# Linear attention with a routed expert layer in float32: two matmuls per chunk cut to 64x64 and 128x64 tiles of the array

## Chip, cores and metric

The kernel runs on one core of a Trainium2 chip. The metric is device time of one execution in microseconds (us). Before the change the median of 3 runs is 420.43 us (419.73 to 420.62).

## What is computed

Two layers follow each other. The first is causal linear attention with a decay per head (4 batches, 8 heads, 768 positions, 64 dimensions), with a state that goes from block to block; the second routes each of the 3072 tokens to one of 8 experts and runs that expert's two matrices.

```python
for b in range(nb):                                    # along the sequence
    intra = einsum('bhic,bhjc->bhij', qb, kb) * Dmask  # scores, with the decay
    intra = einsum('bhij,bhjd->bhid', intra, vb)
    inter = einsum('bhid,bhde->bhie', qb * lam_pow, kv_state)
    out[:, :, sl] = intra + inter
    kv_state = lam_block * kv_state + einsum('bhsd,bhse->bhde', kb * rev_pow, vb)
x = out, heads side by side                            # 3072 tokens of 512
e = argmax(x @ w_gate + modality_bias)                 # one expert for each token
y = gate * relu(x @ w1[e]) @ w2[e]
```

## The kernel before

**Attention.** The kernel takes the sequence in chunks of 128 positions: 6 per batch, 24 in all, and all 8 heads of a chunk together, as 4 pairs. In what follows a chunk has a number g from 0 to 23, and g % 6 is its place in the batch. The loop over g (`for g in range(0, ng + 2)`, from L730) is written as a pipeline, so that one turn works on three chunks. On TensorE (PE) a turn has five blocks of float32 matmuls, and the profile shows each such matmul as two passes:

- scores of chunk g (L224): keys times queries, for each pair and each head 64 rows of the array (one head's dimensions) and all 128 columns. Two heads go to two halves of the rows. The results are two tiles `s` in PSUM (three buffers in turn), one for the first heads of the pairs and one for the second.
- from the state, chunk g-1 (L262): 64x64 tiles, four side by side. Left out where g-1 begins a batch.
- outputs of chunk g-1 (L273): masked scores times values, 128 rows by 64 columns, two tiles side by side.
- carry of chunk g (L239): what the chunk adds to the state, 128 rows by 64 columns. Left out where g ends a batch.
- tokens of chunk g-2 (L285): the outputs are turned so that tokens stand in rows, and times the gate's weights, with all 128 rows and 128 columns of the array. The result goes to PSUM tiles `x` (two buffers).

VectorE (DVE) makes `pt`, the masked scores (L227, two per chunk, one for each tile `s`), `qd` and `kd`, decayed queries and keys (L204, L209), the state (L243, L248), the sum of the logits (`lg`, L289) and, once a batch, the routing. ScalarE (ACT) copies outputs and tokens out of PSUM (L275, L286). SyncE (SP) issues loads of 2 MB, one for two chunks (L182), into three buffers; the load of chunk pair n is issued when the outputs of chunk 2n-5 have read the last of the buffer that it goes to. Once a batch 7 small bf16 matmuls rank the tokens (`route_places`, L330 to L335), and once 1 counts tiles (L369).

The five blocks are written in this order, but a scheduler sets each engine's order from the dependencies and its own durations; an engine then takes its instructions in that order and waits at the one whose input is missing.

**Experts.** From some 116 us on the tokens of one expert are gathered in tiles of 256, and each float32 product is done as three matmuls of split operands (`three`, L588 to L592). Weights are split on ACT and DVE (`split`, L520, L521). The last chunk's tokens block stands among the first matmuls of the experts.

Of the kernel before, what the change touches and what calls it, by code (L numbers as in the profile page):

```python
# [15 lines left out]
P = 128  # L16
# [6 lines left out]
E, DM, F = 8, 512, 1024  # L23
# [15 lines left out]
def linear_attention_moe(tc, qkv, lam, modality, wg, mbias, w1, w2, out):  # L39
    nc = tc.nc  # L40
    with ExitStack() as ctx:
# [78 lines left out]
        iw = const.tile([P, NP, P + E], F32, name="iw")  # L120
# [50 lines left out]
        halves2 = [slice(hl * D, (hl + 1) * D) for hl in range(2)]  # L171
# [17 lines left out]
        def loaded(g):  # L189

            t = halves[g // HB][:, :, g % HB]
            kt, qt = (t[:, i].rearrange("p (a t) -> p a t", a=NP) for i in range(2))
            return kt, qt, t[:, 2], t[:, 3]
# [23 lines left out]
        def scores(g):  # L217
            kt, qt, vt, kn = loaded(g)
            pts = []
            sps = [ps.tile([P, NP, P], F32, name="s", bufs=3),  # L220
                   ps.tile([P, NP, P], F32, name="x", bufs=2) if g == 1 else ps.tile([P, NP, P], F32, name="s", bufs=3)]
            for p in range(NP):
                for hl, r in enumerate(halves2):
                    nc.tensor.matmul(sps[hl][:, p, :], kt[r, p, :], qt[r, p, :], start=True, stop=True)  # L224
            for hl in range(2):
                pt = work.tile([P, NP, P], F32, name="pt", bufs=4)
                op = nc.vector.tensor_tensor(out=pt, in0=sps[hl], in1=dk[:, hl], op=ALU.mult)  # L227
                pts.append(pt)
            return pts, op
# [48 lines left out]
        def tokens(g, xt, lg):  # L278
            c = g % NC
            xn = work.tile([P, NP, P + E], F32, name="xn", bufs=4)  # L280
            for hf in range(2):
                xp = ps.tile([P, 2, 256], F32, name="x", bufs=2)
                for j in range(2):
                    p = hf * 2 + j
                    nc.tensor.matmul(xp[:, j, : P + E], xt[:, p, :], iw[:, p, :], start=True, stop=True)  # L285
                copies.append(nc.scalar.copy(out=xn[:, 2 * hf : 2 * hf + 2, :], in_=xp[:, :, : P + E]))  # L286
            nc.scalar.dma_start(out=xs[g * P : (g + 1) * P, :].rearrange("t (p d) -> t p d", p=NP),
                                in_=xn[:, :, :P])
            logits.append(nc.vector.tensor_reduce(out=lg[:, c, :], in_=xn[:, :, P:].rearrange("p q e -> p e q"),  # L289
                                                  axis=AX, op=ALU.add))  # L290
# [439 lines left out]
        for g in range(0, ng + 2):  # L730
# [4 lines left out]
            if g < ng:  # L735
                st1[g], masked = scores(g)
# [15 lines left out]
            if g >= 2:  # L752
                b, c = divmod(g - 2, NC)
                if c == 0:
                    lgs[b] = work.tile([P, NC, E], F32, name="lg", bufs=2)
                tokens(g - 2, st2.pop(g - 2), lgs[b])
                if routed is not None:
                    slots = route_places(*routed)
                    routed = None
                if c == NC - 1:  # L760
                    routed = (b, *route(b, lgs.pop(b)))
# [30 lines left out]
        hl = [work.tile([P, 2, TT], F32R, name=f"hl{i}", tag=t, bufs=3) for i, t in enumerate(("qd", "qd", "kd", "kd"))]  # L792
# [154 lines left out]
```

## Time and profile before

| | |
|---|---|
| median of 3 runs | 420.43 us |
| profiled execution | 419.86 us |
| its span, first to last instruction | 418.1 us |
| PE busy | 404.6 us (97% of the span) |
| DVE busy | 245.9 us (59%) |
| ACT busy | 188.4 us (45%) |
| GpSimd (POOL) busy | 100.0 us (24%) |
| read from HBM, written | 90.97 MB, 13.68 MB |
| stage of attention | up to some 116 us |

The page lists each engine's busy time; a matmul's end is modelled, so a busy PE says that it always had work, not that the work was dense. How dense it is shows in the timeline: it gives each block's start, and the distance from one block's start to the next can be set against the number of passes in the block. PE's granted clock is 0.996 of full speed over the span.

### The profile page before, as it was taken

The page shows a single profiled execution, that of the slowest core. Times are in us where ns is not written, and L with a number is a line of the kernel's source. Part 1 is how long each engine was busy: PE and PEld are TensorE (multiplying, and loading weights), DVE is VectorE, ACT ScalarE, POOL GpSimd, SP SyncE. Part 2 cuts the span into 40 slices and gives each one's busy share as a digit, 9 for nine tenths or more (in the row PEclk, how much of TensorE's full clock was granted, in tenths as well). Part 3 has the DMA queues.
Part 4 walks back from the last instruction along what each step waited for, and adds up shares of the span by engine and source line. Part 5 has one row for each costly group of instructions (what it writes and reads, how often), then busy time and mean ns, then how long its engine had stood idle before and what let it go on. Part 6 is the DMA issues. An engine that isn't in the chain of part 4 may idle for free.

```text
span 418.1 us, 9536 instructions
## 1 busy us (share of the span) xinstructions
PE 404.6 (97%) x3665; PEld 356.4 (85%) x3666; DVE 245.9 (59%) x487; ACT 188.4 (45%) x298; POOL 100.0 (24%) x110
## 2 busy tenths in 40 slices
PE   8999999999979999999999999999999999999993
PEld 4687888888879888689898989899998989898982
DVE  4594967788369952168393745638190927456240
ACT  1213343233378151258392736546381927365330
POOL 3110143522540741050322030212121120300001
PEclk9999999999999999999999999999999999999998
DMA  4999989899940039101206567711111020200101
GB/s 145 396 335 381 349 295 330 277 313 318 393 141 3 2 109 401 55 18 45 75 28 184 183 210 250 230 51 52 52 33 69 2 76 27 67 27 2 52 1 48
DMA packets 35093, 63.01 MB, mean 151 GB/s; under 512 B 7381, under 2 KB 21213, under 8 KB 35040
## 3 DMA queue, kind: packets, MB, share of 16 engines
q1 hardware_dynamic: 17056, 43.08, 29.8%
q0 software_dynamic: 4768, 12.69, 9.1%
q10 hardware_dynamic: 13216, 6.56, 5.3%
q8 instruction: 30, 0.49, 0.5%
q14 instruction: 23, 0.19, 0.2%
HBM read 90.97 MB, written 13.68 MB: 250 GB/s over the span
## 4 chain that ended last, share of the span: by engine, by line
issue 44%; PE 22%; DMA 13%; POOL 8%; DVE 6%; POOLq 3%; SPq 3%; ACT 1%; DVEq 0%; ACTq 0%
PE s L224 6%; PE x L285 5%; DMA load<-in_qkv_dram 5%; PE o L273 5%; DMA idx<-inv 4%; POOL out_dram L666 4%; POOL xg L548 3%; DMA xg<-xs,idx 3%; POOLq L844 2%; PE o L262 2%; PE kv L239 2%; DVE w1l L521 1%; SPq L565 1%; DVE w2l L521 1%; PE s L592 1%
## 5 line engine op out<-in xcount | busy, mean ns | idle before, releaser
L588 PE MATMUL s<-xh,w1h 128*128 128x256 f32 x384 | 107.4, 280 | 0.8 <-ACT xh L520 0.8
L592 PE MATMUL s<-xh,w1l 128*128 128x256 f32 x384 | 107.4, 280 | 0.8 <-DVE w1l L521 0.8
L591 PE MATMUL s<-xl,w1h 128*128 128x256 f32 x384 | 107.2, 279 | 0.0
L521 DVE TENSOR_TENSOR w1l<-raw,w1h 128x1024 fp32r<-128x1024 f32 x48 | 58.0, 1218 | 72.6 <-ACT w1h L520 72.6
L588 PE MATMUL o<-w2h,hh 128*128 128x512 f32 x192 | 75.8, 395 | 0.0
L592 PE MATMUL o<-w2h,hl 128*128 128x512 f32 x192 | 74.9, 390 | 0.0
L591 PE MATMUL o<-w2l,hh 128*128 128x512 f32 x192 | 74.8, 390 | 0.0
L588 PEld LDWEIGHTS s<-xh,w1h 128*128 128x128 f32 x384 | 72.2, 188 | 1.6 <-ACT xh L520 1.0
L592 PEld LDWEIGHTS s<-xh,w1l 128*128 128x128 f32 x384 | 72.2, 188 | 1.2 <-DVE w1l L521 1.2
L591 PEld LDWEIGHTS s<-xl,w1h 128*128 128x128 f32 x384 | 72.2, 188 | 0.4
L521 DVE TENSOR_TENSOR w2l<-raw,w2h 128x1024 fp32r<-128x1024 f32 x48 | 58.3, 1217 | 2.0 <-ACT w2h L520 2.0
L520 ACT CAST w1h<-raw 128x1024 fp32r<-128x1024 f32 x48 | 50.0, 1055 | 20.6 <-PE s L591 19.8
L520 ACT CAST w2h<-raw 128x1024 fp32r<-128x1024 f32 x48 | 50.1, 1045 | 0.0
L665 ACT ACTIVATE y<-o,idx 128x512 f32<-128x512 f32 x20 | 13.8, 690 | 75.9 <-PE o L592 45.9
L666 POOL DMA_INDIRECT out_dram<-y,idx x20 | 20.3, 1014 | 114.8 <-ACT y L665 99.4
L607 DVE SCALAR_TENSOR_TENSOR hl<-s,hh 128x512 fp32r<-128x512 f32 x48 | 32.8, 684 | 22.3 <-ACT hh L606 22.3
L592 PEld LDWEIGHTS o<-w2h,hl 128*128 128x128 f32 x192 | 36.0, 188 | 7.6
L591 PEld LDWEIGHTS o<-w2l,hh 128*128 128x128 f32 x192 | 36.1, 188 | 7.2
L588 PEld LDWEIGHTS o<-w2h,hh 128*128 128x128 f32 x192 | 36.1, 188 | 7.1
L548 POOL DMA_INDIRECT xg<-xs,idx x20 | 24.6, 1228 | 72.7 <-PE x L581 68.8
L275 ACT COPY xt<-o 128x256 f32<-128x256 f32 x48 | 17.8, 372 | 49.7 <-PE o L273 45.6
L606 ACT ACTIVATE hh<-s 128x512 fp32r<-128x512 f32 x48 | 28.7, 597 | 19.8 <-PE s L592 19.6
(190 smaller groups left out, 487.4 us busy)
## 6 DMA issues: line engine op xcount, KB each, us to landing
raw<-in_w_dram SPq DMA_DIRECT2D x104, 512.0 KB
load<-in_qkv_dram SPq DMA_DIRECT2D x11, 2048.0 KB
xs<-xn ACTq DMA_DIRECT2D x24, 256.0 KB
load<-in_qkv_dram SPq DMA_DIRECT2D x4, 512.0 KB
spare<-in_w_dram SPq DMA_DIRECT2D x4, 512.0 KB
w1h<-in_w_dram SPq DMA_DIRECT2D x4, 512.0 KB
inv<-pad SPq DMA_DIRECT2D x2, 196.0 KB
inv<-pad SPq DMA_DIRECT2D x2, 192.0 KB
```

Source lines behind the costliest of these rows:

```text
L224: nc.tensor.matmul(sps[hl][:, p, :], kt[r, p, :], qt[r, p, :], start=True, stop=True)
L273: mm = nc.tensor.matmul(op[half][place(p, hl), i, :], vt[:, (2 * p + hl) * D : (2 * p + hl + 1) * D], pts[hl][:, p, :], start=(c == 0 and ...
L285: nc.tensor.matmul(xp[:, j, : P + E], xt[:, p, :], iw[:, p, :], start=True, stop=True)
L520: cp = nc.scalar.copy(out=hi, in_=src)
L521: df = nc.vector.tensor_tensor(out=lo, in0=src, in1=hi.bitcast(F32), op=ALU.subtract)
L548: last = nc.gpsimd.indirect_dma_start(out=(to or xg)[t][:m], out_offset=None, in_=xs[:rows, :], in_offset=bass.IndirectOffsetOnAxis(ap=idx ...
L588: mm = nc.tensor.matmul(out, ah, bh, start=first, stop=False)
L591: nc.tensor.matmul(out, ah, bl, start=False, stop=False)
L592: return nc.tensor.matmul(out, al, bh, start=False, stop=last)
L606: act = nc.scalar.activation(out=hh[i], in_=hp, func=AF.Relu)
L607: nc.vector.scalar_tensor_tensor(out=hl[i], in0=hp, scalar=0.0, in1=hh[i].bitcast(F32), op0=ALU.max, op1=ALU.subtract)
L666: sc = nc.gpsimd.indirect_dma_start(out=out, out_offset=bass.IndirectOffsetOnAxis(ap=idx[:, t, 0:1], axis=0), in_=y, in_offset=None, bound ...
```

## The change

Two loops get one more level. The scores of one head are no longer one matmul of 64 rows and 128 columns, but two of 64 rows and 64 columns, for the two halves of the key positions; so a chunk's scores have 16 matmuls in place of 8, on four tiles of the array. The tokens block is cut the same way along its columns: 8 matmuls of 128 rows and 64 columns in place of 4 of 128 by 128. The number of columns that each matmul streams (128 and 136) stays. Operands, results and everything else in the program stay too; the two new lines move the line numbers behind them by one and two.

```diff
             for p in range(NP):
                 for hl, r in enumerate(halves2):
-                    nc.tensor.matmul(sps[hl][:, p, :], kt[r, p, :], qt[r, p, :], start=True, stop=True)
+                    for s in halves2:
+                        nc.tensor.matmul(sps[hl][s, p, :], kt[r, p, s], qt[r, p, :], start=True, stop=True)
...
                 for j in range(2):
                     p = hf * 2 + j
-                    nc.tensor.matmul(xp[:, j, : P + E], xt[:, p, :], iw[:, p, :], start=True, stop=True)
+                    for r in halves2:
+                        nc.tensor.matmul(xp[r, j, : P + E], xt[:, p, r], iw[:, p, :], start=True, stop=True)
```

The tilings of a turn, block by block, are 64x128, 64x64, 128x64, 128x64 and 128x128 before; with the change they are 64x64, 64x64, 128x64, 128x64 and 128x64.

The scheduler's order changes in two ways. The first is on PE, at the routing of a batch. Before, from the tokens of chunk 6 on (a row is a group of matmuls, out<-in and the output's shape; `load` is q, k and v):

```order
L285 MATMUL x<-iw,xt 128x136 x4
L224 MATMUL s<-load 128x128
L330 LDWEIGHTS lowb
L330 MATMUL x<-oh,lowb 128x48
L333 LDWEIGHTS onesb
L333 MATMUL x<-ohsum,onesb 128x48
...
L335 MATMUL x<-oh,onesb 128x8
L224 MATMUL s<-load 128x128 x7
L262 MATMUL o<-qd,state_117 64x128 x8
```

Now:

```order
L287 MATMUL x<-iw,xt 64x136 x8
L332 LDWEIGHTS lowb
L332 MATMUL x<-oh,lowb 128x48
L335 LDWEIGHTS onesb
L335 MATMUL x<-ohsum,onesb 128x48
...
L337 MATMUL x<-oh,onesb 128x8
L225 MATMUL s<-load 64x128 x16
L263 MATMUL o<-qd,state_117 64x128 x8
```

The routing (and the count of L369) has moved from behind the first matmul of the scores to directly behind the tokens.

The second is on DVE: of the two `kd` of a newly loaded chunk pair, the second has moved forward. Before, from the masked scores of chunk 9 on; the first `kd` is that of chunk 12 and waits for the load of chunks 12 and 13, the second that of chunk 13, and the masked scores between them are those of chunk 10:

```order
L227 TENSOR_TENSOR pt<-s,dk 128x512 x2
L204 TENSOR_TENSOR qd<-load,pq 128x512
L248 TENSOR_TENSOR state_116<-faded,kv 128x256
L289 TENSOR_REDUCE lg<-xn 128x8
L209 TENSOR_TENSOR kd<-load,dk 128x512
L227 TENSOR_TENSOR pt<-s,dk 128x512 x2
L204 TENSOR_TENSOR qd<-load,pq 128x512
L209 TENSOR_TENSOR kd<-load,dk 128x512
L248 TENSOR_TENSOR state_117<-faded,kv 128x256
```

Now:

```order
L228 TENSOR_TENSOR pt<-s,dk 128x512 x2
L204 TENSOR_TENSOR qd<-load,pq 128x512
L249 TENSOR_TENSOR state_116<-faded,kv 128x256
L291 TENSOR_REDUCE lg<-xn 128x8
L209 TENSOR_TENSOR kd<-load,dk 128x512 x2
L228 TENSOR_TENSOR pt<-s,dk 128x512 x2
L204 TENSOR_TENSOR qd<-load,pq 128x512
L249 TENSOR_TENSOR state_117<-faded,kv 128x256
```

Both `kd` now stand ahead of the masked scores of chunk 10. The same holds at the load of chunks 18 and 19, ahead of the masked scores of chunk 16; there the order before was

```order
L404 TENSOR_SCALAR deltaA<-ntA 1x8
L384 TENSOR_TENSOR tmpA<-tri,ntA 1x64
L209 TENSOR_TENSOR kd<-load,dk 128x512
L385 TENSOR_REDUCE endsA<-tmpA 1x8
L227 TENSOR_TENSOR pt<-s,dk 128x512
L388 TENSOR_TENSOR pastA<-sidx,endsA 1x16
L227 TENSOR_TENSOR pt<-s,dk 128x512
```

and is now

```order
L209 TENSOR_TENSOR kd<-load,dk 128x512
L406 TENSOR_SCALAR deltaA<-ntA 1x8
L386 TENSOR_TENSOR tmpA<-tri,ntA 1x64
L209 TENSOR_TENSOR kd<-load,dk 128x512
L387 TENSOR_REDUCE endsA<-tmpA 1x8
L228 TENSOR_TENSOR pt<-s,dk 128x512
L390 TENSOR_TENSOR pastA<-sidx,endsA 1x16
L228 TENSOR_TENSOR pt<-s,dk 128x512
```

The second `kd` and two small instructions of the tile list have come between the waiting `kd` and the masked scores. At the load of chunks 8 and 9 `qd` and `kd` of chunk 9, which stood behind the masked scores of chunk 7, stand ahead of them now, and at the loads of chunks 14 and 15 and of 20 and 21 the waiting `qd` stands ahead of the masked scores of chunk 12 and 18, behind which it stood. The orders of ACT, POOL and SP are what they were.

## Rows read from the trace of the kernel before

**Rows 1.** The page of the profile: busy time, share of the span and instructions of each engine, and the line of PE by slice (tenths of busy time; 40 slices of 10.45 us).

```profile
PE 404.6 (97%) x3665; PEld 356.4 (85%) x3666; DVE 245.9 (59%) x487; ACT 188.4 (45%) x298; POOL 100.0 (24%) x110
...
PE   8999999999979999999999999999999999999993
```

**Rows 2.** The view by stretch, two stretches of the attention stage: length, busy time of each engine in us (with the number of instructions), granted clock of PE, share of time in which the DMA engines were busy, GB/s.

```profile
36.60:46.30 9.70, 9.70 (x162) 8.59 (x162) 7.60 (x15) 3.04 (x8) 1.00 (x2) 1.00 1.03 365
46.30:55.60 9.30, 9.30 (x157) 8.17 (x153) 7.93 (x29) 2.97 (x9) 3.50 (x5) 1.00 0.97 337
```

**Rows 3.** The timeline of PE, two steady chunks, the second by its first block alone: start in us, length in us, engine, line, operation, tiles and shape. A row takes in all instructions of a block (x16 is 8 float32 matmuls of two passes); the next row starts where the next block starts. The last row is the block with which the chunk after ends.

```profile
62.01 1.16 PE L224 MATMUL s<-load 64*128 64x128 f32 x16
63.10 0.67 PE L262 MATMUL o<-qd,state 64*64 64x128 f32 x16
63.70 1.09 PE L273 MATMUL o<-pt,load 128*64 128x128 f32 x16
64.62 0.64 PE L239 MATMUL kv<-load,kd 128*64 128x64 f32 x16
65.18 1.19 PE L285 MATMUL x<-iw,xt 128*128 128x136 f32 x8
66.31 1.16 PE L224 MATMUL s<-load 64*128 64x128 f32 x16
...
70.01 1.16 PE L224 MATMUL s<-load 64*128 64x128 f32 x16
```

**Rows 4.** What passes cost without a switch between them, and whether weight loads lie beside them: the timeline of PE in the thin tile of 32 rows (four column tiles), the group of that line among the groups by line (busy us, mean ns of one), and the timeline of the weight loads for the block of outputs that starts at 63.70.

```profile
179.98 1.95 PE L644 MATMUL o<-spare,hnt 128*32 128x128 f32 x64
...
L644 PE MATMUL o<-spare,hnt 128*32 128x128 f32 x64 | 2.0, 274 | 0.1
...
63.69 0.85 PEld L273 LDWEIGHTS o<-pt,load 128*64 128x64 f32 x16 [0.17 <-issue]
```

**Rows 5.** A chunk with routing matmuls: the timeline of PE, and of ACT for the copies out of the tokens block that starts at 47.77.

```profile
48.89 0.49 PE L224 MATMUL s<-load 64*128 64x128 f32 x2
49.31 0.20 PE L330 MATMUL x<-oh,lowb 128*128 128x48 bf16 x1
...
53.87 1.16 PE L224 MATMUL s<-load 64*128 64x128 f32 x16
...
48.54 0.85 ACT L286 COPY xn<-x 128x272 f32<-128x272 f32 x2
```

**Rows 6.** The timeline of DVE where it waits for a load of q, k and v (in brackets: us idle before, and what ended it), and the rows behind.

```profile
42.30 0.69 DVE L204 TENSOR_TENSOR qd<-load,pq 128x512 f32<-128x512 f32 x1 [2.00 <-DMA load<-in_qkv_dram]
...
43.63 1.28 DVE L227 TENSOR_TENSOR pt<-s,dk 128x512 f32<-128x512 f32 x2
...
56.74 0.69 DVE L209 TENSOR_TENSOR kd<-load,dk 128x512 f32<-128x512 f32 x1 [2.13 <-DMA load<-in_qkv_dram]
57.34 1.28 DVE L227 TENSOR_TENSOR pt<-s,dk 128x512 f32<-128x512 f32 x2
...
81.51 0.70 DVE L209 TENSOR_TENSOR kd<-load,dk 128x512 f32<-128x512 f32 x1 [0.49 <-DMA load<-in_qkv_dram]
82.13 0.20 DVE L385 TENSOR_REDUCE endsA<-tmpA 1x8 f32<-1x64 f32 x1
82.26 0.67 DVE L227 TENSOR_TENSOR pt<-s,dk 128x512 f32<-128x512 f32 x1
...
82.94 0.67 DVE L227 TENSOR_TENSOR pt<-s,dk 128x512 f32<-128x512 f32 x1
...
86.41 1.27 DVE L227 TENSOR_TENSOR pt<-s,dk 128x512 f32<-128x512 f32 x2
...
90.88 0.69 DVE L204 TENSOR_TENSOR qd<-load,pq 128x512 f32<-128x512 f32 x1 [0.45 <-DMA load<-in_qkv_dram]
```

**Rows 7.** The timeline of PE: the first block of chunk 6, and the blocks that the rows of the group before lead to (scores of chunk 8; outputs of chunks 7, 10, 16 and 18).

```profile
36.59 1.16 PE L224 MATMUL s<-load 64*128 64x128 f32 x16 [0.98 <-DMA load<-in_qkv_dram]
...
44.59 1.16 PE L224 MATMUL s<-load 64*128 64x128 f32 x16
...
46.28 1.09 PE L273 MATMUL o<-pt,load 128*64 128x128 f32 x16
...
59.86 1.09 PE L273 MATMUL o<-pt,load 128*64 128x128 f32 x16
...
85.80 1.09 PE L273 MATMUL o<-pt,load 128*64 128x128 f32 x16
...
93.34 1.09 PE L273 MATMUL o<-pt,load 128*64 128x128 f32 x16
```

**Rows 8.** The timeline of SP: the issues of the loads of chunk pairs 6 and 9.

```profile
47.42 0.37 SPq L182 DMA_DIRECT2D load<-in_qkv_dram  x1
...
72.84 0.37 SPq L182 DMA_DIRECT2D load<-in_qkv_dram  x1
```

**Rows 9.** The way from attention into the experts, by engine: PE at the last tokens block, the ACT copy of its second half, the DVE split behind it, and PE as it takes that up.

```profile
119.47 0.73 PE L285 MATMUL x<-iw,xt 128*128 128x136 f32 x4 [0.99 <-DVE xl L521]
...
123.96 0.38 PE L592 MATMUL s<-xh,w1l 128*128 128x256 f32 x1 [0.38 <-DVE w1l L521]
...
120.94 0.39 ACT L286 COPY xn<-x 128x272 f32<-128x272 f32 x1 [0.32 <-PE x L285]
...
122.69 1.22 DVE L521 TENSOR_TENSOR w1l<-raw,w1h 128x1024 fp32r<-128x1024 f32 x1
```

## The prediction

> **What bounds the kernel now.** I read the page first: PE is busy for 97% of the span, in every slice but two for 90% or more [rows 1]. That alone does not say that PE sets the time, since a stalled stream of matmuls also counts as busy. [...] The timeline of PE then shows how dense the work is: one turn of the loop takes 66.31 - 62.01 = 4.30 us, and a turn without the state block 70.01 - 66.31 = 3.70 us [rows 3]. Last, the timeline of DVE shows where loads end a wait: at 42.30, 56.74, 81.51 and 90.88 DVE starts the moment that a load of q, k and v lands [rows 6].
>
> **What a switch of tiling costs.** The longest run of passes without a switch has 64 on four tiles: (1.95 - 0.274) / 63 = 26.6 ns per pass of 128 columns [rows 4], so 53.2 ns on two tiles and 106 on one. By that a turn's passes take: scores 16 x 53.2 = 0.85, state 16 x 26.6 = 0.43, outputs 0.85, carry (64 columns) 0.43, tokens 8 x 106 x 136/128 = 0.90; together 3.46. The turn's 4.30 leaves 0.84 for four switches, 0.21 each. A second way: the turn without the state block is 0.60 shorter [rows 3]; its passes are 0.43, and it has one switch less, so a switch is 0.17. Where the tiling stays, from outputs to carry, the distance is 0.92 against passes of 0.85; where it changes, from state to outputs, 0.60 against 0.43. I take 0.18, nearer to the second, which compares two turns alike in all else; bounds 0.17 and 0.21.
>
> **The change, part by part.** *Scores and tokens themselves.* Scores become 32 passes on four tiles, 32 x 26.6 = 0.85; tokens 16 on two, 0.90. The passes cost what they cost before. I add 0.02 per turn for scores: their row has 16 passes from 62.01 in 1.16, outputs 16 in 1.09 [rows 3]. As to the weight loads, twice as many: in the outputs block 16 of them take 0.85 us, as long as the passes beside them [rows 3, 4], so they hide. [...]
>
> *Switches per turn.* 4 become 2: a full turn saves 2 x 0.18 + 0.02 = 0.38. A turn without the state block has 3 before and 2 now: 0.20. A turn without the carry goes from outputs to tokens, a switch before and none now: 4 to 2, again 0.38. The three routings and the one count lose one switch (0.18), but now stand directly behind tokens and need the `x` buffer whose copy starts at 48.54 and is half of 0.85 long, so free at 48.97, against 48.89 where PE could start [rows 5]: 0.18 - 0.08 = 0.10 each.
>
> *Until chunk 6: nothing.* Its scores start at 36.59 after 0.98 of waiting for a load [rows 7]; I take that landing as fixed, so that what is saved earlier turns into a longer wait.
>
> *Chunk 6 to the outputs of chunk 10: lost.* DVE takes its instructions in order, and the new order puts `qd` and `kd` of two chunks ahead of the masked scores behind them. At 42.30 four of them (0.60 each, the distance of two starts at 56.74 and 57.34) and the small `lg` (0.12) come first: masked scores of chunk 7 start at 44.8, not 43.63, and the first is done 0.68 later, at 45.5 [rows 6]. The third matmul of chunk 8's scores writes the buffer that this frees. Behind it lie 28 passes (0.75), state (0.43) and a switch (0.18): outputs of chunk 7 start at 46.9, not 46.28 [rows 7]. Their end issues load 6 (47.42 now) [rows 8], which comes up to 0.6 later; with the queue full, 0 to 0.6 of it may reach the landing, and I take all: 57.3 in place of 56.74. Then two `kd` (1.20), the masked scores (0.68) and again 0.75 + 0.43 + 0.18: outputs of chunk 10 start at 60.5, against 59.86: 0.7 late.
>
> *Then up to the outputs of chunk 16.* Saved: 0.18 for the rest of turn 11, 4 x 0.38 for turns 12 and 14 to 16, 0.20 for turn 13, 0.20 for turn 17 up to its outputs block, and 2 x 0.10 for a routing and the count: 2.3, so 1.6 ahead. But load 9, issued behind the outputs of chunk 13 (72.84) [rows 8], is only some 0.26 earlier by then (-0.7 + 0.18 + 0.38 + 0.20 + 0.20), and lands at 81.25. Behind it now lie 0.75 (as from 81.51 to 82.26), the second `kd` 0.60 and two small ones, 0.13 each by the row of `endsA`; the masked scores start at 82.9, end at 83.5 [rows 6], and 0.75 + 0.43 + 0.18 later the outputs of chunk 16 start at 84.9. That is 0.9 ahead of 85.80 [rows 7], not 1.6.
>
> *To the end of attention.* The masked scores of chunk 17 come 3.47 after the second of chunk 16 (82.94 to 86.41 [rows 6]), now 0.60 less, and hold PE for some 0.15. Saved: 0.18, then turns 18 to 23 with 5 x 0.38 + 0.20, the last state block's 0.18 and one routing 0.10: 2.56. So attention ends 0.9 + 2.56 - 0.15 = 3.3 earlier.
>
> *Into the experts.* The last tokens block stands among 128x128 matmuls, and its new tiling adds four switches. Two of them lie ahead of the copy at 120.94, on which the sum of logits, the routing's first steps and the split at 122.69 follow, for which PE waits at 123.96 [rows 9]: 0.36 lost; the others fall into that wait. From there on PE is full [rows 1] and everything it waits for hangs on its own progress, so the rest moves along.
>
> **Sum.** 3.3 - 0.36 = 2.9 saved. The profiled execution took 419.86, its span 418.1; 419.86 - 2.9 = 417.0. The median of the runs lies 0.57 above it: **417.5**. Its own range: the far end if loads 9 and 10 come no earlier (outputs of chunk 18 then start at 90.88 + 0.60 + 0.68 + 0.75 + 0.18 = 93.1, 0.25 ahead of 93.34 [rows 6, 7], and 0.18 + 4 x 0.38 + 0.18 + 0.10 - 0.36 = 1.6 follow: 1.9 saved, 418.5); and 416.5 with load 6 not delayed (0.5, as it brings load 9 that much forward) and 14 switches at 0.21 behind load 9 (0.4).
>
> **Rivals.**
> *The loads follow the faster PE and DVE keeps up.* Then all turns from chunk 6 on save: 15 x 0.38 + 3 x 0.20 + 0.18 + 0.40 = 6.9, less 0.36: 413.9. For it: each load is issued by PE's own outputs. Against: the DMA engines are busy for 0.97 and more of these stretches [rows 2], and the new DVE order waits earlier. Chance 0.15.
> *Not the tiling costs, but each change of block.* Five blocks stay five, nothing is gained, and the DVE waits stay hidden in the slack: 420.4. For it: the blocks differ in more than their tiling. Against: outputs to carry is 0.92 with 0.07 over its passes, a new block at nearly no cost [rows 3]. Chance 0.10.
> *Slower: four tiles do not run side by side for a whole scores block.* The tiles of one head now share rows of queries and come as neighbours. If they went two at a time, at the 53.2 ns of two tiles, scores would take 1.70: 0.85 more against 0.38 less, some 9 us over 18 turns: 429. It decides from (0.85 + 0.38) / 32 = 38 ns per pass on. Against it: 26.6 ns held for 64 passes whose four tiles share all rows [rows 4], and the state block takes 0.60 [rows 3]. [...] Chance 0.06.
>
> **How the numbers follow.** The forecast has 0.69, of which 0.10 is the case of unmoved loads. Some 0.84 us (0.2%) is what a measurement of this kernel can tell from no change, so faster means under 419.6. Faster: 0.82 (0.67 from the forecast, 0.15 from the first rival); within: 0.12 (0.10 from the second rival, 0.02 from the forecast); slower: 0.06. The range leaves out the second and third rivals and a little (0.04) of the first: 414.6 to 419.4.
>
> **What would show it.** Right: a full turn of 3.9 us in the timeline of PE with switches only ahead of scores and of outputs; scores in 0.85 us; new waits of PE for `pt` in the scores of chunks 8, 11 and 17; attention over by 113. Wrong: turns of 3.9 with no such waits (first rival), turns of 4.3 (second), scores of over 1.2 us (third), or a wait of PE on the gathered rows of the first expert tile, which must be there 3 us earlier.

## The result, and the profile after

The forecast was wrong. The changed kernel took 422.81 us in the median of 13 runs, the kernel before 420.12 us beside it: a ratio of 1.0064 (95% interval 1.0039 to 1.0088), slower, where 417.5 us was forecast. In a second comparison, on another chip, it was 426.41 against 420.41 us, 1.0154 (1.0118 to 1.0189). The profiled execution took 421.71 us. Medians are of all executions, ratios leave out slow ones at a lower granted clock, among them one of the kernel before at 665.29 us (clock 0.557) and one of chunk_pads_tokens (below) at 611.12 (0.604).

The page after, against [rows 1]: busy time and instructions of the engines, PE's busy time by slice, and the granted clock by slice.

```profile
PE 399.3 (95%) x4242; PEld 351.2 (84%) x4242; DVE 246.6 (59%) x487; ACT 188.0 (45%) x298; POOL 100.2 (24%) x110
...
PE   8897889899979999999999999999999999999994
...
PEclk9999999999989999999999999999999999999999
```

PE has 577 more matmul records and 5 us less busy time. It now has holes in the first third, the attention stage, and a lower clock at the way into the experts (0.84 of full speed in the slice from 115.5 us on).

The blocks themselves do what was forecast. PE in a steady turn, against [rows 3]:

```profile
50.41 1.10 PE L225 MATMUL s<-load 64*64 64x128 f32 x32
51.34 0.62 PE L263 MATMUL o<-qd,state 64*64 64x128 f32 x16
51.88 1.09 PE L274 MATMUL o<-pt,load 128*64 128x128 f32 x16
52.81 0.64 PE L240 MATMUL kv<-load,kd 128*64 128x64 f32 x16
53.27 1.10 PE L287 MATMUL x<-iw,xt 128*64 128x136 f32 x16
54.30 1.10 PE L225 MATMUL s<-load 64*64 64x128 f32 x32
```

A turn takes 54.30 - 50.41 = 3.89 us, 0.41 less than before. The time went into what lies between the turns. PE's waits from 20 to 126 us (engine and line that waited, for what, us in total, times, longest):

```profile
PE s L225 <- DVE pt L228: 3.6, 4, 1.6
PE s L225 <- DMA load<-in_qkv_dram: 3.0, 2, 2.4
PE o L274 <- issue: 1.7, 1, 1.7
PE x L583 <- DMA xg<-xs,idxA: 1.6, 1, 1.6
```

Before, the same stretch had no wait for `pt`, none for gathered rows and none with the releaser "issue" (PE waits, and nothing in the profile holds it); loads cost 1.4. Where these waits lie, in the timeline of PE, against [rows 7]:

```profile
37.15 1.10 PE L225 MATMUL s<-load 64*64 64x128 f32 x32 [2.35 <-DMA load<-in_qkv_dram]
...
46.20 0.98 PE L225 MATMUL s<-load 64*64 64x128 f32 x26 [1.27 <-DVE pt L228]
...
47.66 1.09 PE L274 MATMUL o<-pt,load 128*64 128x128 f32 x16
...
60.27 0.98 PE L225 MATMUL s<-load 64*64 64x128 f32 x26 [1.65 <-DVE pt L228]
...
61.73 1.09 PE L274 MATMUL o<-pt,load 128*64 128x128 f32 x16
...
83.65 0.66 PE L274 MATMUL o<-pt,load 128*64 128x128 f32 x8 [1.70 <-issue]
...
87.91 1.09 PE L274 MATMUL o<-pt,load 128*64 128x128 f32 x16
...
118.86 0.98 PE L583 MATMUL x<-ident,xg 128*128 128x128 f32 x7 [1.60 <-DMA xg<-xs,idxA]
```

SP issues loads 6, 9 and 11 later, the first two against [rows 8] (load 11 before: 90.78):

```profile
48.80 0.37 SPq L182 DMA_DIRECT2D load<-in_qkv_dram  x1
...
74.14 0.37 SPq L182 DMA_DIRECT2D load<-in_qkv_dram  x1
...
93.86 0.38 SPq L182 DMA_DIRECT2D load<-in_qkv_dram  x1
```

And PE's granted clock falls behind the wait for gathered rows (first row: a stretch of 4 us, columns as in [rows 2]). The second row is the same stretch of a second profile of the kernel before: there is no such wait there, and the clock falls too.

```profile
120.00:124.00 4.00, 3.58 (x21) 2.44 (x22) 1.29 (x2) 1.30 (x5) 2.07 (x2) 0.64 0.70 201
```

```profile
120.00:124.00 4.00, 4.00 (x23) 4.00 (x24) 2.21 (x9) 2.77 (x5) 1.12 (x2) 0.60 0.61 170
```

The first expert tile scales its output at 141.95, 2.78 us later than in the first profile before and 1.48 later than in the second (140.47); the next one is 1.89 later than in the first, and so it stays to the end.

### The profile page after: what moved, and what is told of

Same layout as the page of the kernel before. It is cut to its first block, busy times and chain, and to the rows that moved or that the text cites. A ratio compares the mean times of both kernels' runs of the same rounds, so it can differ in the third digit from the quotient of the medians.

```text
span 420.0 us, 10687 instructions
## 1 busy us (share of the span) xinstructions
PE 399.3 (95%) x4242; PEld 351.2 (84%) x4242; DVE 246.6 (59%) x487; ACT 188.0 (45%) x298; POOL 100.2 (24%) x110
## 4 chain that ended last, share of the span: by engine, by line
issue 45%; DMA 23%; PE 9%; DVE 8%; POOL 8%; SPq 3%; POOLq 3%; ACT 0%; DVEq 0%
DMA load<-in_qkv_dram 12%; DMA idx<-inv 4%; POOL out_dram L668 4%; POOL xg L550 3%; DMA xg<-xs,idx 3%; PE s L225 3%; POOLq L846 2%; PE o L274 2%; PE x L287 2%; DMA xg<-xs,idxA 2%; DVE w1l L523 2%; SPq L567 1%; DMA raw<-in_w_dram 1%; PE o L263 1%; DVE kd L209 1%
```

## Experiments

Three theories. **A**: the new DVE order makes PE wait for masked scores behind loads, so loads are issued later, and all behind them. **B**: PE runs out of instructions, since a turn has 48 float32 matmuls where it had 36 (a third more; the 1.6 times in the expectation below is wrong). **C**: a late load 3 was an accident of the transfers. Medians are compared with the kernel before in the same comparison. "Without a releaser" sums PE's waits with the releaser "issue" from 20 to 115 us of one profile, or to the end of attention where that comes earlier; the last column is the start of the first transpose of the first expert tile, the end of attention.

| run | matmuls, switches per turn | median us (runs) | ratio to before (interval) | without a releaser, us | attention ends |
|---|---|---|---|---|---|
| before, first profile | 36, 4 | | | 0 | 116.19 |
| before_again | 36, 4 | 420.22 (1) | | 0 | 116.56 |
| the change, first profile | 48, 2 | 422.81 (13) | 1.0064 (1.0039 to 1.0088) | 1.7 | 116.93 |
| change_again | 48, 2 | 426.41 (6) | 1.0154 (1.0118 to 1.0189) | 3.4 | 119.91 |
| dve_order_before | 48, 2 | 424.21 (6) | 1.0107 (1.0070 to 1.0143) | 2.3 | 118.32 |
| masked_first | 48, 2 | 422.06 (12) | 1.0037 (1.0004 to 1.0070) | 3.7 | 117.15 |
| old_masked_first | 36, 4 | 421.09 (12) | 1.0022 (1.0000 to 1.0044) | 0.8 | 118.91 |
| scores_only | 44, 3 | 421.07 (11) | 1.0039 (1.0015 to 1.0063) | 0 | 118.24 |
| scores_masked_first | 44, 3 | 422.34 (12) | 1.0042 (1.0013 to 1.0072) | 1.9 | 121.42 |
| tokens_only | 40, 3 | 420.17 (12) | 1.0000 (0.9970 to 1.0030) | 0 | 116.34 |
| tokens_masked_first | 40, 3 | 419.95 (12) | 0.9980 (0.9956 to 1.0003) | 0.7 | 115.41 |
| no_loads_old | 36, 4 | 449.70 (4) | 1.0711 (1.0679 to 1.0744) | 0 | 114.97 |
| no_loads_new | 48, 2 | 442.54 (4) | 1.0531 (1.0493 to 1.0569) | 0.7 | 107.03 |
| chunk_loads_old | 36, 4 | 417.73 (12) | 0.9939 (0.9919 to 0.9960) | 0 | 114.72 |
| chunk_loads_new | 48, 2 | 421.87 (12) | 1.0034 (1.0009 to 1.0059) | 2.3 | 118.20 |
| chunk_pads_old | 36, 4 | 422.67 (12) | 1.0011 (0.9973 to 1.0050) | 0 | 114.76 |
| chunk_pads_scores | 44, 3 | 423.01 (12) | 1.0014 (0.9981 to 1.0047) | 2.5 | 115.28 |
| chunk_pads_tokens | 40, 3 | 414.40 (6) | 0.9846 (0.9808 to 0.9885) | 0.2 | 111.48 |
| chunk_pads_new | 48, 2 | 419.62 (12) | 0.9960 (0.9927 to 0.9993) | 6.6 | 115.90 |

### The changed kernel a second time

No edit.

> The changed kernel as it is, for a second profile and a second set of times. Every theory: 421.5 to 423.5 us. What it tells: which of the stretches that the first profile of the changed kernel lost are lost each time. Theory A (the new DVE order makes PE wait for masked scores, the loads of q, k and v are issued later, and all behind them) says that the waits of 1.3 us in the scores of chunk 8 and of 1.6 us in those of chunk 11 are there again, within 0.3. Theory B (PE runs out of instructions, since the change has 1.6 times as many per chunk) says that a wait of PE like the 1.7 us in the outputs of chunk 15, for which the profile shows no releaser, is there again, there or in another block of attention. Theory C (an accident of the transfers: load 3 came 0.6 us late) says that load 3 lands before 36.7 us this time, and that what follows is earlier by as much.

The wait in the scores of chunk 8 was there (1.5 us), that of chunk 11 only 0.3. Load 3 landed in time (scores of chunk 6 at 36.18), as C says, and the run was slower all the same: C does not explain the loss. What came back is the stall without a releaser, in more pieces. PE in the state block of chunk 15 and its outputs:

```profile
80.96 0.45 PE L263 MATMUL o<-qd,state 64*64 64x128 f32 x3 [0.37 <-issue]
81.69 0.46 PE L274 MATMUL o<-pt,load 128*64 128x128 f32 x4 [0.28 <-issue]
82.41 0.27 PE L274 MATMUL o<-pt,load 128*64 128x128 f32 x1 [0.27 <-issue]
83.12 0.55 PE L274 MATMUL o<-pt,load 128*64 128x128 f32 x4 [0.44 <-issue]
83.83 0.37 PE L274 MATMUL o<-pt,load 128*64 128x128 f32 x1 [0.16 <-issue]
84.55 0.89 PE L274 MATMUL o<-pt,load 128*64 128x128 f32 x5 [0.34 <-issue]
```

The block's inputs are there, since its first passes have run, and it takes from 81.69 to 85.07 where [rows 3] has 0.92. Its pieces start 0.71 to 0.72 us apart. Meanwhile the transfers have thinned out (DMA share, last column but one, of 0.49, then 0.12 and 0.05), so these holes are not explained by transfer engines that are full at that moment. Behind them the granted clock falls:

```profile
82.00:83.00 1.00, 0.41 (x5) 0.00 (x0) 0.00 (x0) 0.00 (x0) 0.69 (x2) 1.00 0.49 128
83.00:84.00 1.00, 0.72 (x5) 0.42 (x5) 0.77 (x1) 0.00 (x0) 0.97 (x2) 0.86 0.12 35
84.00:85.00 1.00, 0.66 (x5) 0.46 (x5) 1.00 (x4) 0.12 (x1) 0.62 (x1) 0.50 0.05 5
...
84.00:88.00 4.00, 3.65 (x47) 3.28 (x50) 4.00 (x15) 1.27 (x4) 1.81 (x2) 0.61 0.26 61
```

### DVE's order: dve_order_before, masked_first, old_masked_first

```diff
# dve_order_before (the changed kernel): kd and qd behind masked scores as in the kernel before
+        pt_of, hold = {}, {9: 7, 13: 10, 14: 12, 19: 16, 20: 18}
...
+            if after is None and g in hold:
+                after = pt_of[hold[g]]
...
+            pt_of[g] = op
# masked_first (the changed kernel), old_masked_first (the kernel before)
-            if 1 <= g < ng - 1:
-                st0[g + 1] = prepare(g + 1)
...
                 st1[g], masked = scores(g)
+            if 1 <= g < ng - 1:
+                st0[g + 1] = prepare(g + 1, None if g + 1 == 18 else masked)
```

> The changed kernel, with the order on DVE held as it was before the change at the five places where it had moved: kd and qd of chunks 9, 13, 14, 19 and 20 behind the masked scores of chunks 7, 10, 12, 16 and 18. PE, ACT, POOL and SP keep the orders of the changed kernel. Theory A: the waits of PE for masked scores go (1.27, 1.65 and 0.39 us), each load behind them is issued 1 to 1.5 us earlier, and the kernel takes 2 to 3 us less than the changed one: 419.5 to 421, no slower than the kernel before. Theory B (instructions): it takes what the changed kernel takes, 422 to 423.5. The forecast's own sum without the lost stretches (the switches alone) would be 416.5 to 418.

> The changed kernel, with kd and qd of each chunk behind the masked scores of the chunk before it, so that DVE never waits for a load ahead of masked scores that PE waits for (kd of chunk 18 alone stays where it was, since SP's order would move otherwise). Orders of PE, ACT, POOL and SP as in the changed kernel. Theory A: outputs of chunks 7, 8, 10, 13 and 14 no longer hang on the load that lands in their turn, loads 6 and 9 are issued earlier than in the kernel before, and the time is another 1 to 2 us under that of the run with the DVE order of before: 417.5 to 420. A rival to that, transfers at their rate (the DMA engines are busy for 0.97 and more of the stretch before the change, so that an earlier issue brings no earlier landing): as the run with the order of before, within 0.5 us. Theory B: 422 to 423.5.

> The kernel before with its own tilings, and the same edit of the DVE order as in the run masked_first: the two have the same DVE order to the instruction, so they differ by the tilings alone. What the tilings are worth once DVE's order is no matter: if a switch of tiling costs what the forecast says and PE sets the pace, this run is 2 to 3 us slower than masked_first. If the loads set the pace, the two are alike within 0.7 us. If the doubled instructions cost (theory B), this run is the faster of the two by 1 us or more. Against the kernel before: 0 to 2 us less.

With the order of before, the change took 2.20 us less, which is not clear of noise (the intervals, 1.0070 to 1.0143 and 1.0118 to 1.0189, overlap); PE still waited 1.8 us for `pt` there. With masked scores first it took 4.35 less, clear of noise, and PE had no wait for `pt`, while it stood as long without a releaser as in change_again (3.7 against 3.4). So A is a part. But neither came under the kernel before, and with one DVE order in both the old tilings took 421.09 and the new 422.06, a difference within the noise: the switches saved nothing that stayed. masked_first has 3.7 us without a releaser. Its times follow the mean granted clock: three runs at 0.997 and 0.998 took 419.6 to 420.5, five at 0.979 to 0.989 took 423.0 to 426.0.

### Each half alone: scores_only, tokens_only, scores_masked_first, tokens_masked_first

The diff of the change, one half of it; the last two with the edit of masked_first.

> The kernel before with the first half of the change: scores on four 64x64 tiles, tokens as before on the whole array. A turn has three switches of tiling (before four, the change two) and 44 float32 matmuls (before 36, the change 48). The DVE order of the chunks' instructions is that of the changed kernel in all places. The forecast's sum, were switches all: 1.4 us less than before. Theory A (DVE order, loads issued late): as slow as the changed kernel or 0 to 2 us slower than it, since it has its DVE order and one switch more, so 1.5 to 2% over the kernel before by the last runs. Theory B (PE runs out of instructions): between before and change, 0.7 to 1.2% over before, with fewer stretches of PE without a releaser than the change has (9 to 12 in its two profiles of attention).

> The kernel before with the second half of the change: tokens on two 64-column tiles, scores as before. Three switches per turn, 40 float32 matmuls. The DVE order is that of before but for one kd each at the loads of chunks 12 and 13 and qd of chunk 9. The forecast's sum: 1.4 us less than before. Theory A: it keeps the wait in the scores of chunk 11 and half of that of chunk 8, so 0 to 0.7% over before. Theory B: 40 matmuls per turn are near the 36 of before, so 0 to 0.4% over it, with 0 to 4 stretches without a releaser.

> Scores on four tiles, tokens on the whole array (44 float32 matmuls per turn, three switches), and DVE's order as in masked_first and old_masked_first, to the instruction. It stands between the two (48 matmuls and two switches; 36 and four). If what masked_first lost against old_masked_first (1 us by the medians) is PE without instructions, this run has none of those stretches in attention, as scores_only had none, and takes no more than old_masked_first (at most 0.2% over the kernel before). If it is the switches or the tiling itself that costs, it lies between the two (0.3% over before).

> Tokens on two tiles, scores as before (40 matmuls per turn, three switches), DVE's order as in masked_first. tokens_only was no slower than the kernel before in spite of 3.4 us in which PE waited for masked scores behind a load. With these waits gone (theory A), 0.2 to 0.6% faster than the kernel before, that is 417.7 to 419.5. If the landing of the loads sets the pace whatever DVE's order is, the same as before within 0.2%.

scores_only was faster than A and B said (1.5 to 2% and 0.7 to 1.2% over before): with the change's DVE order and a switch more than the change it lost 0.4%, and had no stall without a releaser. scores_masked_first had 1.9 us of them, against expectation, and a load 3 that PE waited 4.2 us for. Tokens alone cost nothing; with masked scores first they may be 0.2% faster (the interval just takes in no change).

### Without the loads: no_loads_old, no_loads_new

```diff
-                halves[LOADS - 1 + g // HB] = load_half(LOADS - 1 + g // HB)
+                halves[LOADS - 1 + g // HB] = halves[(LOADS - 1 + g // HB) % LOADS]
```

> The kernel before, with loads 3 to 11 left out: chunks from 6 on take the data of the first three loads again, so that 18 MB less is read and no chunk from 6 on waits for its data; the routing then sees other tokens, so the expert part may have another length than in the kernel before, but the same as in no_loads_new. It shows attention at the pace of the engines alone: full turns of 4.30 us on PE, attention over 3 to 8 us earlier than in the kernel before (at 116), if transfers hold it there.

> The changed kernel, with loads 3 to 11 left out in the same way; DVE's order of the chunks' instructions is the same in this and in no_loads_old but for the places of three small ones. If transfers (and the waits behind them) took away what the tilings save, then without them the saving is there: full turns of 3.9 us, and 5 to 7.5 us less than no_loads_old. Theory B in its strong form (instructions come too slowly for 48 matmuls in 3.9 us whatever else is transferred): stretches without a releaser as in the changed kernel, and a difference of under 3 us. Theory B in its weak form (instruction fetches wait behind data in the transfer engines) says as the first: hardly any such stretch here.

Chunks from 6 on work on the data of the first loads here, so the routing sees other tokens and the expert part is longer; the two runs are compared with each other alone. 449.70 - 442.54 = 7.16 us: here the tilings give about what the forecast's first rival worked out (6.9 less 0.36). One turn of each, old and new, from scores to scores:

```profile
52.64 1.16 PE L224 MATMUL s<-load 64*128 64x128 f32 x16
...
56.94 1.16 PE L224 MATMUL s<-load 64*128 64x128 f32 x16
```

```profile
57.11 1.10 PE L225 MATMUL s<-load 64*64 64x128 f32 x32
...
60.99 1.10 PE L225 MATMUL s<-load 64*64 64x128 f32 x32
```

4.30 and 3.88. With 48 matmuls in 3.88 us PE has 0.7 us without a releaser in all, so the pace alone does not make the holes; they came with the loads running. (Without loads the old tilings end attention at 114.97, 1.2 before the kernel before: there PE, not loads, holds attention nearly all of the way.)

### Loads chunk by chunk: chunk_loads_old, chunk_loads_new

With the edit of masked_first (for all chunks), the first loads and the second expert matrices' tiles cut to fit, and

```diff
-HB = 2
-LOADS = 3
+HB = 1
+LOADS = 6
...
-            return qkv[divmod(g, NC // HB)].rearrange("x p c f -> p x c f")
+            return qkv[divmod(g, NC // HB)]
...
-        "qkv": c(_np.stack([cols(kr), cols(inputs["q"]), rows(vr), rows(kr)], axis=2)),
+        "qkv": c(_np.stack([cols(kr), cols(inputs["q"]), rows(vr), rows(kr)], axis=3)),
```

> The changed kernel with DVE's order as in masked_first, and q, k and v loaded chunk by chunk: six buffers of 1 MB in place of three of 2 MB (the same memory, the same bytes, 8 KB of one partition next to each other in HBM). The load of chunk n is issued when outputs of chunk n-6 are done, so half of each old load is issued a turn (some 4 us) earlier. If the time is lost because a load is issued so late that PE waits for its landing, while the transfer engines stand still for 10 to 20% of the stretch in between (their share is 0.79 to 0.91 from 55 to 86 in the changed kernel), then most of the 7 us that the tilings save without loads comes back: 414 to 418 us. If the rate of the transfers sets the pace: 420 to 423, as masked_first.

> The same loads chunk by chunk and the same DVE order, with the tilings of the kernel before. If late loads are what holds the changed kernel: here PE sets the pace with its turns of 4.30 us and gains little from earlier loads, 418 to 420, so 2 to 6 us more than chunk_loads_new. If the rate of the transfers sets the pace: as chunk_loads_new within 1 us.

The other way round: the old tilings gained 0.6%, the new ones lost. In chunk_loads_new, ACT and PE at the first routing:

```profile
39.81 0.85 ACT L289 COPY xn<-x 128x272 f32<-128x272 f32 x2 [0.55 <-PE x L288]
47.52 0.52 ACTq L290 DMA_DIRECT2D xs<-xn  x1
48.08 0.24 ACT L350 ACTIVATE l<-l 128x48 f32<-128x48 f32 x1 [7.42 <-DMA xs<-xn]
```

```profile
49.20 0.20 PE L333 MATMUL x<-oh,lowb 128*128 128x48 bf16 x1 [5.08 <-ACT xn L289]
...
51.25 1.08 PE L264 MATMUL o<-qd,state 64*64 64x128 f32 x16
52.26 1.85 PE L275 MATMUL o<-pt,load 128*64 128x128 f32 x16
53.94 0.63 PE L241 MATMUL kv<-load,kd 128*64 128x64 f32 x16
```

ACT stood from 40.7 to 47.5 at the issue of one store of tokens. The program has eight semaphores for such transfers, in turn; by the trace this store's was that of an earlier store of tokens (issued at 31.73), which landed only at 47.44. The next runs take it for that of a fill of the table of places (`inv<-pad`); but the four fills had all landed by 32.2. ACT's copies waited behind it, and PE, in order, behind the routing that needs an `x` buffer. The clock fell (0.63 of full speed on average from 46.3 to 55.6 us), so that state and outputs took 1.01 and 1.68 us where a turn before they took 0.54 and 0.93.

### The same without that wait: chunk_pads_new, chunk_pads_old, chunk_pads_tokens, chunk_pads_scores

```diff
-                    behind(nc.sync.dma_start(out=dst, in_=pad[:, : dst.shape[1]]), tables)
+                    behind(nc.gpsimd.dma_start(out=dst, in_=pad[:, : dst.shape[1]]), tables)
```

> As chunk_loads_new (tilings of the change, 48 matmuls per turn, loads chunk by chunk, masked scores first), with the four fills of the table of places issued from POOL's queue, so that no store of tokens waits behind one of them. The stall of 5.1 us in the first routing and the fall of the clock behind it should go. If late loads were the whole loss: 413.5 to 416 us, 2 us or more under chunk_pads_old. If PE runs out of instructions: 417 to 420, no faster than chunk_pads_old, with several stretches without a releaser in attention.

> As chunk_loads_old (tilings of before, 36 matmuls per turn), with the four fills issued from POOL's queue. It had no such stall on PE, so 416.5 to 418, as chunk_loads_old; it is the one that chunk_pads_new and chunk_pads_tokens are compared with.

> The same with tokens on two tiles and scores as before (40 matmuls per turn, three switches). By the switches alone, 18 turns of 0.18 us less: 3 us under chunk_pads_old, 413.5 to 415. If instructions are short already with 40: as chunk_pads_old or over it.

> As chunk_pads_tokens, but with scores on four tiles and tokens on the whole array: three switches per turn as there, 44 float32 matmuls per turn in place of 40. By the switches it would take what chunk_pads_tokens takes, 414 to 415 us. If the number of instructions counts, it has stretches of PE without a releaser behind fetches of instructions, fewer or shorter than the 6.6 us that chunk_pads_new has in attention, and takes 415.5 to 418.

Moving the fills also moves the turn of the semaphores, and these four profiles show no wait of ACT for a store of tokens; that the fills had caused it is not shown. In chunk_pads_new nothing but B is left to hold PE: waits for loads are 0.2 us, for masked scores none, for a copy 0.4. Its waits from 20 to 115 us, and four of the places:

```profile
PE o L264 <- issue: 2.9, 6, 0.9
PE s L226 <- issue: 2.4, 4, 1.1
PE kv L241 <- issue: 0.8, 1, 0.8
```

```profile
31.80 0.45 PE L264 MATMUL o<-qd,state 64*64 64x128 f32 x8 [0.93 <-issue]
...
43.92 0.45 PE L264 MATMUL o<-qd,state 64*64 64x128 f32 x8 [0.81 <-issue]
...
50.39 0.63 PE L241 MATMUL kv<-load,kd 128*64 128x64 f32 x15 [0.77 <-issue]
...
56.58 1.10 PE L226 MATMUL s<-load 64*64 64x128 f32 x32 [0.69 <-issue]
```

Some 1.5 us ahead of each of these four holes the transfer records have one fetch on instruction queue 8, of 16 KB, and from one such fetch to the next it is some 6.3 us. The match is not complete: by its record each of these fetches is over some 0.5 us before the hole begins, the fetches at 35.27 and 59.28 have no hole behind them, and the two holes at 80 and 81 us have no fetch within 3 us ahead. Nor do the loads make the fetch itself longer: 0.9 to 1.1 us here, 0.9 to 1.5 in no_loads_new. With 40 matmuls PE has 0.2 us of such stalls, and the kernel takes 414.40 us, 1.5% less than the one before and 5.2 less than with the whole change (in spite of 2.0 us in which PE waits for a copy at the count). With 44 and the same three switches it has 2.5 us, and attention ends 3.8 us later than with 40. The count differs between these two, but so does the block that has the extra matmuls (scores with 44, tokens with 40); no run keeps the two apart.

The medians of chunk_pads_old and chunk_pads_scores can't be read so: their times fall in two groups (417.3 to 418.1 and 420.3 to 424.2; 417.6 to 419.6 and 422.2 to 424.8), and the profile of chunk_pads_scores, from the upper one, shows a wait of 3.4 us in the experts, for the gathered rows of a thin tile, long after attention. Why these rows come late in some runs stays open. By the lowest times 40 matmuls are first too (414.18); 48 come next (415.69), since with their two switches they gain more (7.16 without the loads) than 6.6 us of holes take away, and 36 and 44 are alike (417.33 and 417.55). Attention ends at 114.76 with 36 and at 115.28 with 44.

### The kernel before a second time

No edit.

> The kernel before as it is, for a second profile: 419 to 422 us. With 36 matmuls per turn, PE has no stretch of 0.4 us or more without a releaser in attention, as in its first profile, or at most one or two.

No wait without a releaser up to 115 us, as in the first profile.

## Why the prediction was wrong, point by point

Starts of PE blocks in us (outputs of a chunk; the last column as in the table above):

| | chunk 7 | 10 | 13 | 16 | 18 | attention ends |
|---|---|---|---|---|---|---|
| before, two profiles | 46.28, 45.78 | 59.86, 59.42 | 71.70, 71.26 | 85.80, 85.83 | 93.34, 93.37 | 116.19, 116.56 |
| forecast | 46.9 | 60.5 | | 84.9 | | 3.3 earlier |
| change, two profiles | 47.66, 46.92 | 61.73, 60.50 | 73.00, 72.16 | 87.91, 89.21 | 95.18, 96.17 | 116.93, 119.91 |
| no_loads_old, no_loads_new | 45.05, 43.15 | 58.63, 55.16 | 70.47, 65.92 | 84.57, 78.10 | 92.11, 85.50 | 114.97, 107.03 |

- *What a switch costs; switches per turn*: right. 3.89 for a full turn (forecast 3.92), 3.45 for a short one (41.04 to 44.49; forecast 3.50).
- *Scores and tokens themselves*: right. 0.93 and 1.03 us to the next block, weight loads hidden: they took 0.86 (32 of them) and 0.90 us (16), beside the passes.
- *Routing*: it stands directly behind tokens and cost 0.24 (50.17 to 50.41); the new place was harmless here, and cost 5.1 in chunk_loads_new.
- *Until chunk 6: nothing*: the landing taken as fixed is not: 0.56 later in the first profile, 0.4 earlier in the second. In the first, SP waited 1.1 us ahead of load 3 for a store of tokens with the same semaphore.
- *Chunk 6 to the outputs of chunk 10: lost*: right in kind and place; the forecast's 60.5 is the second profile to 0.01. The first is 1.23 later: load 3 was 0.56 late, and load 6 landed at 58.32 where 57.3 was forecast.
- *Then up to the outputs of chunk 16*: **this step failed**, at load 9, which it had landing at 81.25, 0.26 earlier than before. It landed at 84.09 and 83.23, when DVE's wait for it ended, and outputs of chunk 16 started at 87.91 and 89.21 in place of 84.9. DVE's wait and PE's scores of chunk 17 in the first profile, then in the second:

```profile
84.09 0.77 DVE L209 TENSOR_TENSOR kd<-load,dk 128x512 f32<-128x512 f32 x1 [3.28 <-DMA load<-in_qkv_dram]
...
86.45 0.98 PE L225 MATMUL s<-load 64*64 64x128 f32 x26 [0.39 <-DVE pt L228]
```

```profile
83.23 0.92 DVE L209 TENSOR_TENSOR kd<-load,dk 128x512 f32<-128x512 f32 x1 [2.49 <-DMA load<-in_qkv_dram]
...
87.74 1.10 PE L225 MATMUL s<-load 64*64 64x128 f32 x32
```

Load 9 was issued at 74.14 and 73.31, 1.56 and 0.73 later than forecast (1.23 and nothing of it from the outputs of chunk 10), and took 9.95 and 9.92 us to land where the forecast kept the 8.67 of before; why it took longer stays open. Part of the late issue is a term that the step left out: masked scores of chunk 12 stand behind load 7 now, DVE waited for it until 66.50 and 65.66, and from the outputs of chunk 10 to those of chunk 13 it took 11.27 and 11.66 us where the forecast has 10.88.

In the first profile load 9 alone sets the outputs of chunk 16: the first masked scores of chunk 16 were done 2.3 us behind its landing, and PE, although it had stood 1.70 us without a releaser in the outputs of chunk 15, still waited 0.39 for them. In the second PE was later than the masked scores (no wait at 87.74), held by 1.9 us of such holes and by the lower clock behind them.

The holes, which the forecast put at nothing, also made the next load late: outputs of chunk 15 issued load 10 at 84.35 and 85.68 (before 82.64), it landed at 92.81 and 93.75 (before 90.88), and outputs of chunk 18 started at 95.18 and 96.17 (before 93.34).
- *To the end of attention*: late with load 10. Load 11 was issued at 93.86, in the first profile behind register loads on SP that wait (4.5 us) for DVE's tile list.
- *Into the experts*: the forecast's 0.36 was the wrong term. Weights and gathered rows came later with load 11, PE waited 1.60 for the rows (the sign named beforehand), and the clock fell to 0.64 (to 0.60 in the second profile before, so the fall is not the change's alone); 2.78 us late at the first tile, of which 0.9 came back in the second. "The rest moves along" held from there on.
- *Rivals*: the first one's price was right to 0.6 us in the runs without loads. Its condition did not hold, and it is not enough: in chunk_pads_new PE hardly waits for loads, and the holes remain. The slower one (four tiles not side by side) is refuted by 0.93 for scores. None of the rivals was the one that happened.

What the change lost has three parts. Waits for masked scores behind loads, and loads that come later: shown by masked_first (4.35 us). PE without a releaser: shown to be more with more matmuls in a turn (0 to 0.8 us with 36, 0 to 0.7 with 40, 0 to 2.5 with 44, 1.7 to 6.6 with 48, loads running; one profile of each run) and nearly to go without the loads (0 and 0.7). And the lower clock behind both kinds of hole, which in some profiles falls in the kernel before too. That the holes are a wait for the fetch of instructions is inferred from the places of some of them behind fetches, not shown; nor is it shown what in the loads has to do with it. How the loss of one run is divided among the three is not settled either, since the clock falls in some runs and not in others.

## What to carry to other kernels

Cutting matmuls into more tiles buys shorter blocks with more instructions (here a turn of 3.89 us with 48 matmuls for one of 4.30 with 36): count instructions per us of the new pace, not only passes, and look in the profile for waits with the releaser "issue" inside a block whose inputs are there, and for instruction fetches ahead of them. An order that puts an instruction which waits for a load ahead of one that another engine needs makes the load's landing a bound for both (PE waited 3.6 us for `pt` in the first profile of the change, in masked_first not at all); in a chain of loads, each issued by the work on an earlier one, being late is handed on (load 6 was issued 1.38 us later than before, load 9 1.30). Of a change with two halves, take the one that saves a switch for the fewest instructions (here tokens: 4 matmuls more for one switch, where scores take 8), and check that loads can be issued early enough for the pace it brings. An in-order engine that issues stores can be held by an earlier transfer of which it needs nothing but the semaphore (ACT for 6.8 us in chunk_loads_new).

## What the runs showed of the hardware

- PE stood without a releaser, often inside a block whose inputs were there, for 0.2 to 1.7 us at a time, at 48 matmuls (192 instructions: two passes, each a weight load and a matmul) per 3.9 us. The changed page counts 35 packets with 0.57 MB on the instruction queue, 16 KB each. How many instructions a fetch brings is not shown. Where PE held its pace, without loads, fetches came 4.9 to 5.8 us apart (37.7 to 75.5 us of no_loads_new); in chunk_pads_new, with the holes, some 6.3. Whether the holes come from the fetches is not shown.
- The granted clock fell for part of a stretch after PE had stood, at the lowest to 0.50 of full speed: 0.50 from 84 to 85 us of the second profile (0.61 on average from 84 to 88), behind the holes shown there, 0.50 from 121.5 to 124 of the first (0.64 from 120 to 124), behind the wait of 1.60 us, and 0.60 from 120 to 124 of the second profile before, behind waits of 0.8 and 1.0 us. The first profile before had two such waits as well (0.78 and 0.99) and stayed at 1.00 from 120 to 124. Two blocks that ran at the lower clock took 1.9 and 1.8 times as long (chunk_loads_new: 1.01 for 0.54 us, 1.68 for 0.93).
